# Two attention blocks on one core: another hand-written order for TensorE in the first block

## The chip, the cores and the metric

The kernel runs on one core of a Trainium2 chip. The metric is the device time of one execution in microseconds (us). Five engines work beside each other, each through its own queue in order: TensorE (PE) multiplies matrices into PSUM, VectorE (DVE), ScalarE (ACT) and GpSimd (POOL) work elementwise, and SyncE (SP) issues the DMA transfers. They wait for each other through semaphores.

## The reference

Two attention blocks, A and B, work on inputs of their own, and their outputs stand side by side:

```python
B, S, D = 1, 2048, 512            # both blocks
H = 32; Dh = D // H               # 32 heads of 16
qkv = (x @ wqkv).reshape(B, S, 3, H, Dh).transpose(2, 0, 3, 1, 4)
scores = einsum("bhqd,bhkd->bhqk", q, k) * Dh ** -0.5
# A alone: key j counts for query i only where 0 <= i - j < 256
p = softmax(scores)
o = einsum("bhqk,bhkd->bhqd", p, v)
out = o.transpose(0, 2, 1, 3).reshape(B, S, D) @ wo
# result: concatenate([A, B], axis=-1), float32
```

## The kernel before

All is computed to float32's precision: an operand of a projection is split into a rounded part and its rest, and three products stand for one. The heads are taken in groups of four (`g`, 8 groups), the queries in chunks of 512 (`c`, 4 chunks). A pair (g, c) is a unit. Block A has 32 units, block B 32.

The program has a first block, in which all of block A's attention runs together with the projections of A and of B, and a second block, which is B's attention with the output projections. The change touches the first alone. Its work for TensorE comes in kinds, each with a letter:

- `p`: one projection of 512 tokens or 128 value rows on the full array, 12 matmuls of 512 columns one after the other (line 309).
- `g`: a quarter of two projections side by side, one on each half of the array's rows: 12 matmuls as 6 simultaneous pairs (line 444). Four `g` make two projections. They need two PSUM banks until the last quarter.
- `m`: the scores of one query tile of 128 for two heads, from which the row maxima are taken (line 607): two simultaneous half-array matmuls of up to 384 columns into two banks. DVE then masks and reduces them (lines 616 and 617; line 612 for the first two tiles), which frees the banks. The last of these letters are the first maxima of block B (line 561).
- `e`: the same for block B's first unit, on operands loaded early.
- `t`: two transposes of a unit's negated maxima (line 681). ACT evicts them and two DMAs bring them as rows into the operand of the scores.
- `s`: scores of two heads for one step of a unit (line 717), half-array matmuls into two banks. ACT takes the exponential of each head out of PSUM (line 724), and POOL clears what the window masks (line 735).
- `w`: the probabilities of a step times the values (line 764), all 128 rows with 17 columns a head, four heads side by side in a bank of their own.

So `g`, `m`, `e` and `s` use two halves of the array's rows, `p`, `w` and `t` all 128. PSUM has eight banks: seven go round among `p`, `g`, `m`, `t` and `s`, and one is kept for `w`.

A unit is 8 `m`, a `t`, 6 `s` and 3 `w`. The order is written out by hand: `ORDER_A` (lines 75 to 83) is a string of 761 such letters, and `ORDER_P` (lines 60 to 65) names the 96 projections in the order in which `p` and `g` take them. `Bk21` is block B, keys, heads 16 to 23, tokens 512 to 1023; `v` names a row tile of the values instead. The loop at line 1122 takes the letters one by one and emits their instructions. The loads that SP issues are not in the strings: the kernel keeps a list of loads and reckons times for the emitted work (class `Model`), and a load is emitted when its operands and its buffer are ready by that reckoning. So another string also moves the DMAs.

A projection of queries or keys goes on from PSUM: ACT evicts it (line 392), POOL splits it in two instructions (lines 403 and 404) into one of two `st` tiles, SP stores that to DRAM (line 411), and later loads take it by heads into the operands `oq` and `opk` (lines 489 and 473) on which `m` and `s` work. A value projection is evicted by ACT into one of two `vst` tiles (line 508), stored (line 517) and loaded as `vt` (line 525), which `w` reads.

Of the kernel before, what the change touches and what calls it, by code (L numbers as in the profile page):

```python
# [57 lines left out]
FILL = 16  # L58
WARM = 22
ORDER_P = (  # L60
# [4 lines left out]
    "Bq20 Bq12 Bk30 Bk31 Bk10 Bq33 Bq30 Bq31 Bk32 Bq32 Bk33 Bk21 ").split()  # L65
WAKE = 200
GAP_V = 1500
PIECE = 4
# [4 lines left out]


ORDER_A = (
    "pppppppppppmmmmpmmgmgmptmgmgmmpmsgmsgmmpmsgmsgmwtsmgmsgmmpmsgsmgmtwwmmmpsmgmsgmswwmsgmsgmmpmssptwsmg"
    "msgmswsmgsmgmmwwmgmsgmstwmsgmsgmmwtsgmsgmswmsgmsgmswmmmpssmtwwmspmsmwssmgsmgmswtmsgsmgmwsmswssmwmmmp"
    "mtmswmsswmsmpsmmpsmwtmmmpsmswmmspmsmwsmsmwwtmsmsmsmpmsmtwsmsmwsmmswssmwmmspmmswsmwtsmgmsgmswsmgsmtgm"
    "mwsmwsmmswsmsmpsmmwmswtmsmwsmmmpmsssmmwsmsmwtmmmpsmswmsmsmwtsmsmwsmmpmmswsmtwmmmpmsgmsgmswtsmgmswpsm"
    "gsmwwmsgmmgmpmsgmsgsmwwtsmgmsgmswsmgsmgmmwtsgsmgsmwwmsgmsgmgsmgmswsmgmmgmwsmwtmsgmsgmswtmsgsmgmswwsm"  # L80
    "gmsgmswsmgsmgsmtwwmmmpmsmpmsmwsmmswtmsgmsgmswsmgsmgsmwmsmtwsmmswssmwmmmpmssmtwswmmmpmsgsmgsmwwmsgsmg"
    "etwmmmpmsgmsgmswsegsmgegesgmswsmgesgemtwmmpmsmwmswmsgsmgestwmsgesgmmpemmpmsmwwtemmpsmgmsgsmwmgegsewm"
    "mmpesstwmgmsgeswsmgsmgsmwesgsmgsmwmgsmgmswesmpsmmwtwmmmpmmmwp")
LAND = 400
LAND_V = 0
LGAP = 2500
# [1303 lines left out]
```

## Time and profile before

| what | value |
|---|---|
| median of 3 runs | 1776.09 us (1775.74 to 1776.34) |
| profiled execution: its own time, and its span | 1775.31 us, 1773.6 us |
| TensorE busy | 1756.7 us, 99% of the span |
| VectorE, ScalarE, GpSimd busy | 1527.2, 1402.7 and 650.5 us |
| first projection to the second block's first matmul | 6.60 to 514.88 us |
| granted TensorE clock | 1.00 throughout |

The lines of the profile group instructions by the line of the kernel, the engine and the tiles that they write and read. A row of the timeline is a start, a length, the engine, the line, the tiles, the shape and how many instructions were merged. A matmul's end is modelled and matmuls overlap, so TensorE looks busy nearly all the time, its short waits too. What it really takes is read from one start to the next.

### The profile page before, as it was taken

Reading aid. Unit: us, or ns where it says so; the run is one execution under the profiler, and the core shown is the slowest. Engines: PE = TensorE matmul, PEld = TensorE weight load, DVE = VectorE, ACT = ScalarE, POOL = GpSimd, SP = SyncE. Lnnn points to the kernel's source line nnn. Section 1 sums busy time; section 2 is a strip of 40 time slices with the busy share of each in tenths; the row PEclk is TensorE's granted clock in tenths of the full one; section 3 lists DMA queues with packets and bytes.
Section 4 is the critical chain, followed back from the end, with each engine's and each line's share of the span. In section 5 each row is a group of like instructions: output and inputs, shape, how many; then the busy total and the mean of one; then the engine's idle time right before and its main releaser. Section 6 shows DMA issues by size and latency. Waiting matters only on the chain.

```text
span 1773.6 us, 38893 instructions
## 1 busy us (share of the span) xinstructions
PE 1756.7 (99%) x14783; PEld 912.8 (51%) x14783; DVE 1527.2 (86%) x2386; ACT 1402.7 (79%) x2749; POOL 650.5 (37%) x1334
## 2 busy tenths in 40 slices
PE   8999999999999999999999999999999999999999
PEld 6776657767764444444444444444444344444446
DVE  4756786677789999999999999999999999999921
ACT  4366776665569888888889999999999999999894
POOL 0378888665755441222210123231102322121420
PEclk9999999999999999999999999999999999999999
DMA  8866767645663223111310311120031131010012
GB/s 261 203 204 202 213 206 224 176 147 170 196 182 107 67 85 89 41 41 41 83 37 17 77 29 30 49 60 17 17 78 35 30 65 38 17 39 25 20 44 102
DMA packets 129355, 166.78 MB, mean 94 GB/s; under 512 B 23205, under 2 KB 59045, under 8 KB 129157
## 3 DMA queue, kind: packets, MB, share of 16 engines
q1 hardware_dynamic: 129168, 164.31, 31.7%
q8 instruction: 116, 1.90, 0.5%
q14 instruction: 71, 0.57, 0.1%
HBM read 94.49 MB, written 68.19 MB: 92 GB/s over the span
## 4 chain that ended last, share of the span: by engine, by line
PE 92%; DVE 4%; ACT 1%; POOL 1%; DMA 1%; issue 1%; SPq 0%; POOLq 0%; ACTq 0%; DVEq 0%
PE ps_all L749 28%; PE ps_all L561 18%; PE ps_all L717 18%; PE ps_all L444 11%; PE ps_all L309 8%; PE ps_all L764 4%; PE ps_all L607 3%; DVE mt L564 3%; ACT p L724 1%; DMA in<-xT_A 1%; DVE nm L617 1%; PE ps_all L681 1%; DVE ps_all L616 0%; SPq L489 0%; DMA ld<-od 0%
## 5 line engine op out<-in xcount | busy, mean ns | idle before, releaser
L724 ACT ACTIVATE p<-ps_all 128x512 f32<-128x512 f32 x2432 | 1263.2, 597 | 202.7 <-PE ps_all L717 129.1
L564 DVE TENSOR_REDUCE mt<-ps_all 128x1 f32<-128x512 f32 (+1 forms) x1658 | 1212.7, 805 | 33.3 <-PE ps_all L561 28.5
L717 PE MATMUL ps_all<-oq,opk 51*128 51x512 f32 (+2 forms) x2752 | 757.3, 401 | 3.7 <-ACT p L724 2.0
L561 PE MATMUL ps_all<-opk,oq 48*128 48x512 f32 x2016 | 660.6, 435 | 0.0
L749 PE MATMUL ps_all<-p,vt 128*17 128x512 f32 (+1 forms) x5488 | 571.0, 490 | 0.0
L717 PEld LDWEIGHTS ps_all<-oq,opk 51*128 51x128 f32 x2752 | 386.0, 185 | 218.5 <-ACT p L724 142.9
L561 PEld LDWEIGHTS ps_all<-opk,oq 48*128 48x128 f32 x2016 | 304.1, 184 | 272.6 <-DVE mt L564 164.7
L735 POOL TENSOR_SCALAR_AFFINE_SELECT p<-p 128x256 f32<-128x256 f32 x480 | 179.9, 410 | 107.7 <-ACT p L724 104.3
L749 PEld LDWEIGHTS ps_all<-p,vt 128*17 128x17 f32 x5488 | 93.6, 95 | 214.1 <-issue 201.3
L616 DVE COPY_PREDICATED ps_all<-mone,ps_all 128x256 f32<-128x256 uint16 x224 | 95.3, 425 | 82.1 <-PE ps_all L607 75.4
L617 DVE TENSOR_REDUCE nm<-ps_all 128x2 f32<-128x512 f32 x224 | 155.2, 693 | 7.7
L633 POOL TENSOR_TENSOR mu<-mt 128x16 f32<-128x16 f32 x31 | 6.9, 223 | 411.4 <-DVE mt L564 411.4
L635 POOL TENSOR_TENSOR mu<-mt,mm 128x16 f32<-128x16 f32 x62 | 13.8, 222 | 388.1 <-DVE mt L564 388.1
L444 PE MATMUL ps_all<-x,w 64*128 64x512 f32 x720 | 119.0, 392 | 0.0
L444 PE MATMUL ps_all<-w_o,x_o 64*128 64x512 f32 x576 | 110.0, 394 | 0.0
L309 PE MATMUL ps_all<-x,w 128*128 128x512 f32 x408 | 102.6, 400 | 1.5 <-ACT x L257 0.8
L764 PE MATMUL ps_all<-p,vt 128*17 128x384 f32 (+2 forms) x1408 | 94.1, 387 | 0.1
L607 PE MATMUL ps_all<-opk,oq 48*128 48x384 f32 (+2 forms) x512 | 91.0, 361 | 1.2 <-DVE nm L617 0.3
L803 POOL TENSOR_TENSOR rd<-ld,minus 128x32 f32<-128x32 f32 x15 | 81.9, 5461 | 19.5 <-DMA ld<-od 19.5
L444 PEld LDWEIGHTS ps_all<-x,w 64*128 64x128 f32 x720 | 84.2, 185 | 8.6
L392 ACT ACTIVATE raw<-ps_all 128x512 f32<-128x512 f32 x56 | 32.3, 596 | 70.2 <-PE ps_all L309 55.3
L309 PEld LDWEIGHTS ps_all<-x,w 128*128 128x128 f32 x408 | 74.1, 188 | 23.8 <-ACT p L724 2.8
(81 smaller groups left out, 1046.6 us busy)
## 6 DMA issues: line engine op xcount, KB each, us to landing
parts<-st SPq DMA_DIRECT2D x64, 512.0 KB
oq<-parts SPq DMA_DIRECT2D x128, 128.0 KB
opk<-parts SPq DMA_DIRECT2D x128, 128.0 KB
od<-ou SPq DMA_DIRECT2D x64, 256.0 KB
vd<-vst SPq DMA_DIRECT2D x32, 272.0 KB
oq<-parts SPq DMA_DIRECT2D x128, 64.0 KB
opk<-parts SPq DMA_DIRECT2D x128, 64.0 KB
t<-od SPq DMA_DIRECT2D x32, 256.0 KB
```

The source lines that it names most:

```text
L309: nc.tensor.matmul(ps, l(u), r(v), start=start and k == 0, stop=stop and k == n - 1)
L444: op = nc.tensor.matmul(ps[a ^ turn], l(u)[rows], r(v)[rows], start=turn == q == 0, stop=turn == 1 and q == 11)
L561: nc.tensor.matmul(ps[:, a - lo], q[rows, 128 * qt:128 * qt + 128], k[rows, kc * QC:kc * QC + QC], start=True, stop=True)
L564: op = nc.vector.tensor_reduce(out=m[:, kc, lo:lo + len(sides), r, qt], in_=ps, axis=AX.X, op=ALU.max)
L607: nc.tensor.matmul(two[:, a, 0:w], opq[b, g, c][rows, r, 128 * qt:128 * qt + 128], opk2(g)[rows, r, t0:t1], start=True, stop=True)
L616: nc.vector.copy_predicated(two[:, :, 256:384], later, two[:, :, 0:128])
L617: op = nc.vector.tensor_reduce(out=m[:, :, r, qt, 0], in_=two[:, :, 128:384], axis=AX.X, op=ALU.max)
L717: nc.tensor.matmul(ps[x][:, col:col + n1], opk2(g)[rows, pr, 128 * k:128 * k + 128], opq[b, g, c][rows, pr, q0:q0 + n1], start=True, stop= ...
L724: op = nc.scalar.activation(p[:, a0 + x, :w], ps[x][:, :w], AF.Exp, scale=SCALE)
L735: nc.gpsimd.affine_select(out=v, in_=v, pattern=[[0, 2], [sign, 128]], compare_op=ALU.is_ge, fill=zero_fill, base=base, channel_multiplier ...
L749: nc.tensor.matmul(o[32 * j:32 * j + VW, q0:q1], vt[(g // 2) % 2][:, kt, vc:vc + VW], pts[1, g, c, kt, j // 2][:, j % 2, q0:q1], start=kt ...
L764: nc.tensor.matmul(o[32 * j:32 * j + VW, q0:q0 + w], vt[(g // 2) % 2][:, kt, vc:vc + VW], pts[b, g, c, m, j // 2][:, j % 2, col:col + w], ...
```

## The change

Both strings are new from a certain letter on. The first 31 letters of `ORDER_A` and the first 16 names of `ORDER_P` stay. Nothing else is changed: there are as many letters of each kind (280 `m`, 192 `s`, 96 `g`, 96 `w`, 48 `p`, 33 `t`, 16 `e`), each projection is named once, and the instructions that they emit are the same in number and size. Counting `w` and `t` as one kind, `p` as another and the half-array letters as a third, the string changes kind 259 times, where it was 242.

```diff
 ORDER_P = (
-    "Aq00 Ak00 Ak01 Av11 Av02 Av03 Aq01 Av01 Ak02 Av21 Av13 Aq02 Av12 Av00 Aq03 Ak03 Av20 Av10 Av33 Ak20 Av32 "
...
+    "Aq00 Ak00 Ak01 Av11 Av02 Av03 Aq01 Av01 Ak02 Av21 Av13 Aq02 Av12 Av00 Aq03 Ak03 Av33 Av32 Av23 Av10 Aq12 "
...
 ORDER_A = (
-    "pppppppppppmmmmpmmgmgmptmgmgmmpmsgmsgmmpmsgmsgmwtsmgmsgmmpmsgsmgmtwwmmmpsmgmsgmswwmsgmsgmmpmssptwsmg"
...
+    "pppppppppppmmmmpmmgmgmptmgmgmmpsmgmsgmmpmsgsmgmwmmtpmsgmsgmswwsmgsmgmtpsmgmsgmswsmgmsgmmwpmmtpsmwsmg"
...
```

Of what the two strings do to TensorE's queue, two places near 196 and 244 us of the execution before are shown. `opk` with `oq` in that order is an `m` (L607), the other way round an `s` (L717), `p_..` with `vt` a `w` (L764), `ident` with `nm` a `t` (L681), `x` with `w_` a projection.

The first place is in TensorE's queue after the values of unit (2, 0)'s second and third step. Before:

```order
L764 MATMUL ps_all<-p_2_0_2_1_2446,vt_78 17x256 x2
L681 LDWEIGHTS nm_74
L681 MATMUL ps_all<-ident,nm_74 32x128
L607 MATMUL ps_all<-opk_75,oq_2_3_2210 128x384 x2
L717 MATMUL ps_all<-oq_2_1_1854,opk_75 128x256 x4
L717 MATMUL ps_all<-oq_2_1_1854,opk_75 128x384 x2
L717 MATMUL ps_all<-oq_2_1_1854,opk_75 128x128 x2
L309 MATMUL ps_all<-x_2_0_239,w_3_0_1298 128x512 x3
```

After the change:

```order
L764 MATMUL ps_all<-p_2_0_1_1_2376,vt_78 17x384 x2
L717 MATMUL ps_all<-oq_2_1_1869,opk_75 128x256 x4
L607 MATMUL ps_all<-opk_75,oq_2_3_2211 128x384 x2
L764 MATMUL ps_all<-p_2_0_2_0_2441,vt_78 17x256 x2
L764 MATMUL ps_all<-p_2_0_2_1_2455,vt_78 17x256 x2
L717 MATMUL ps_all<-oq_2_1_1869,opk_75 128x384 x2
L717 MATMUL ps_all<-oq_2_1_1869,opk_75 128x128 x2
L309 MATMUL ps_all<-x_2_0_239,w_3_1_1238 128x512 x3
```

Rows that repeat are left out. Before, the letters there are `wwtmsmsmsmp`: both `w` together, and then four `m` and three `s` without another kind between them. After, they are `wsmwssmp`: the second `w` stands between an `m` and two `s`.

The second place is in TensorE's queue around the projection after unit (3, 1)'s first `w`. Before:

```order
L607 MATMUL ps_all<-opk_75,oq_4_0_3090 128x128 x2
L717 MATMUL ps_all<-oq_3_1_2604,opk_76 128x384 x2
L717 MATMUL ps_all<-oq_3_1_2604,opk_76 128x128 x2
L717 MATMUL ps_all<-oq_3_2_2732,opk_76 128x128 x2
L717 MATMUL ps_all<-oq_3_2_2732,opk_76 128x384 x2
L607 MATMUL ps_all<-opk_75,oq_4_0_3090 128x256 x2
L764 MATMUL ps_all<-p_3_1_1_0_3170,vt_78 17x256 x2
```

After the change:

```order
L607 MATMUL ps_all<-opk_75,oq_4_0_3084 128x128 x2
L309 MATMUL ps_all<-x_3_0_343,w_3_1_1238 128x512 x3
L717 MATMUL ps_all<-oq_3_1_2613,opk_76 128x384 x2
L717 MATMUL ps_all<-oq_3_2_2743,opk_76 128x128 x2
L717 MATMUL ps_all<-oq_3_2_2743,opk_76 128x384 x2
L607 MATMUL ps_all<-opk_75,oq_4_0_3084 128x256 x2
L764 MATMUL ps_all<-p_3_1_1_0_3166,vt_78 17x256 x2
```

Before, `msssmm` follows the projection up to the next `w`; after, one of the `m` has gone ahead of the projection, and `msssm` follows it.

In the second block TensorE's queue is the same, instruction for instruction.

More of the change, by code (lines that the diff above doesn't have):

```diff
@@ L60 @@
 ORDER_P = (
[4 rows of a table removed]
-    "Bq20 Bq12 Bk30 Bk31 Bk10 Bq33 Bq30 Bq31 Bk32 Bq32 Bk33 Bk21 ").split()
[4 rows of a table added]
+    "Bk13 Bk33 Bk31 Bk32 Bq31 Bq30 Bq11 Bq32 Bq33 Bk10 Bk30 Bq20").split()
 WAKE = 200
@@ L75 @@
 ORDER_A = (
-    "pppppppppppmmmmpmmgmgmptmgmgmmpmsgmsgmmpmsgmsgmwtsmgmsgmmpmsgsmgmtwwmmmpsmgmsgmswwmsgmsgmmpmssptwsmg"
[L77 to L83, printed above, removed]
+    "pppppppppppmmmmpmmgmgmptmgmgmmpsmgmsgmmpmsgsmgmwmmtpmsgmsgmswwsmgsmgmtpsmgmsgmswsmgmsgmmwpmmtpsmwsmg"
+    "msgmswsmgsmgmmtwmgmgmswsmgmsgmswmmswssmgmmgstwmsgsmgmwmmtpsmswwsmmpsmswmsgmsgmswgtmsgmwssmwmsswmsmpm"
+    "mswmsswtmmspmmmpsmswtmmmpsmswmmmpmsmswmsmsmtwsmwssmpmtmswsmsmwsmmswmsmswmmmpsmwtmswssmgsmgmswsmgmsgm"
+    "twssmwmmswsmsmpsmmwstmwmsmwmsmmmpmsssmwmsmtwsmmmpsmstwmsmsmwsmmswsmmpmsmtwmswmmmpsmgsmgmswmsgsmwtpms"
+    "gmswsmgmsgmmwpmsgsmgmwwtmsgmsgmswsmgsmgmswmsgmsgmmwtwsgmsgmgsmgmswsmgmmgmtwmswmsgmsgmswtmsgmsgsmwwms"
+    "gmsgmswsmgsmgmmpmsmwsmtwmsmpmmswsmtwmsgsmgsmwmsgmsgmswmmswtssmswmmmpssmwmsmwsmtwmmmpmsgsmgsmwwmsgsmg"
+    "mtwemmpmsgsmgeswsmgsmgegsmgeswsmgesgmmtwmmpmsmtwsmwsmgmmgswsmgmsgempesswtemmpmswemmpsmgmsgswemgmgmtw"
+    "emmpseswesgmsgsewmgmsgmswmsgesgmswsegmgmswmmspmmswtwmmmpmmmwp")
 LAND = 400
```

6 rows, old and new, of the table ORDER_P are left out of this document.

## The prediction

> **What bounds the kernel now.** I read the page first (engines with busy time, share and instructions), then the chain of work that ended last in two stretches of the first block, then TensorE's timeline there.
>
> ```profile
> span 1773.6 us, 38893 instructions
> ...
> PE 1756.7 (99%) x14783; PEld 912.8 (51%) x14783; DVE 1527.2 (86%) x2386; ACT 1402.7 (79%) x2749; POOL 650.5 (37%) x1334
> ...
> PEclk9999999999999999999999999999999999999999
> ...
> 6.60 0.50 PE L309 MATMUL ps_all<-x,w 128*128 128x512 f32 x1 [0.78 <-ACT x L257]
> ...
> 514.88 0.50 PE L717 MATMUL ps_all<-oq,opk 51*128 51x512 f32 x2
> ```
>
> TensorE bounds it, at full clock. The change can move only what lies between the first projection (6.60 us) and the second block's first scores (514.88): 508.3 us. TensorE's queue in the 1258.7 us behind that is untouched. The matmuls are the same ones, so there are two terms: turns, the time lost where the array passes between whole and halves, and waits, in which the next letter's banks or operands are not ready.
>
> Chain, 190 to 270 us, then 270 to 515.4 us:
>
> ```profile
> by line: PE ps_all L309 20.0%; ACT p L724 14.8%; PE ps_all L717 14.0%; PE ps_all L764 12.4%; PE ps_all L607 9.5%; DVE nm L617 7.9%; PE ps_all L444 5.5%; issue 5.0%; DVE ps_all L616 4.9%; DVE nm L668 1.5%; ACT x L257 1.3%; DVE junk L612 0.9%
> ...
> by line: PE ps_all L444 34.1%; PE ps_all L309 19.3%; PE ps_all L764 18.3%; PE ps_all L717 11.2%; PE ps_all L607 10.4%; PE ps_all L561 4.8%; PE ps_all L681 0.7%; DVE nm L617 0.6%; DVE ps_all L616 0.3%; ACT raw L392 0.2%; issue 0.1%; PE ps_al
> ```
>
> In the earlier stretch the exponentials (L724) and the maxima (L616, L617) hold a good quarter of the chain; later almost nothing. Waits sit where projections are `p`, in lumps of 3 us, and few `g` part the `m` from the `s`.
>
> **Turns.** From start to start on TensorE's timeline:
>
> ```profile
> 163.52 1.06 PE L764 MATMUL ps_all<-p,vt 128*17 128x256 f32 x16
> 164.51 1.04 PE L607 MATMUL ps_all<-opk,oq 48*128 48x384 f32 x6
> ...
> 180.93 1.06 PE L764 MATMUL ps_all<-p,vt 128*17 128x256 f32 x16
> 181.81 0.23 PE L681 MATMUL ps_all<-ident,nm 128*32 128x128 bf16 x2
> 181.97 0.79 PE L607 MATMUL ps_all<-opk,oq 48*128 48x384 f32 x6
> 182.68 3.01 PE L309 MATMUL ps_all<-x,w 128*128 128x512 f32 x12
> 185.62 0.44 PE L717 MATMUL ps_all<-oq,opk 51*128 51x384 f32 x2
> 185.91 0.34 PE L607 MATMUL ps_all<-opk,oq 48*128 48x384 f32 x2
> 186.09 0.34 PE L717 MATMUL ps_all<-oq,opk 51*128 51x384 f32 x2
> 186.35 0.84 PE L764 MATMUL ps_all<-p,vt 128*17 128x384 f32 x8
> ...
> 393.11 0.23 PE L681 MATMUL ps_all<-ident,nm 128*32 128x128 bf16 x2
> 393.13 0.86 PE L764 MATMUL ps_all<-p,vt 128*17 128x384 f32 x8
> ...
> 9.49 17.75 PE ps_all L309 x77
> ```
>
> A 384-column half-array pair takes 0.18 (185.91 to 186.09) among its own kind, 0.29 as the first after a projection (185.62 to 185.91: +0.11) and 0.26 as the last before a `w` (186.09 to 186.35: +0.08). A `w` of four 256-column passes takes 0.88 before a `t` and 0.99 before an `m` (+0.11). A `t` takes 0.16 before an `m`, 0.02 before a `w` (+0.14). A `p` between half-array letters takes 2.94; 77 of its matmuls one after the other (the last row, of the chain) run at 0.23, twelve at 2.77, so its two ends cost some 0.2.
>
> Counting the neighbours in both strings, before to after:
>
> - into halves: from `w` 65 to 78, at 0.22; from `t` 19 to 11, at 0.25; from `p` 35 to 36, at 0.21;
> - out of halves: to `w` 70 to 74 and to `t` 14 to 22, at 0.08; to `p` 35 to 29, at 0.18;
> - among whole-array letters: `t` or `w` to `p` 2 to 8, estimated at 0.22 from the ends of the two (`t` to `p` occurs nowhere before); `p` to `t` 2 to 1, at 0.1; `w` with `t` nothing.
>
> 13 x 0.22 - 8 x 0.25 + 0.21 + 12 x 0.08 - 6 x 0.18 + 6 x 0.22 - 0.1 = +2.2 us. Priced letter by letter to the nanosecond, the turns go from 42.4 to 44.8 us: I take **+2.4**. Where a turn falls ahead of a letter that must wait anyway it costs nothing; the bound below is that half do: +1.2.
>
> [...]
>
> **Waits.** Start to start less the price, over all letters, the waits before come to 31.6 us (434.3 of matmuls, 42.4 of turns and 31.6 make the 508.3): 7.3 in the first 42 letters, which hardly change, 3.8 up to 186 us, 12.8 from there to 279 us, 7.7 behind. What one looks like, inside `smsmsm`:
>
> ```profile
> 195.68 0.44 PE L607 MATMUL ps_all<-opk,oq 48*128 48x384 f32 x2
> 195.96 0.41 PE L717 MATMUL ps_all<-oq,opk 51*128 51x256 f32 x4
> 196.20 0.34 PE L607 MATMUL ps_all<-opk,oq 48*128 48x384 f32 x2
> 196.57 0.38 PE L717 MATMUL ps_all<-oq,opk 51*128 51x256 f32 x1
> 197.19 0.38 PE L717 MATMUL ps_all<-oq,opk 51*128 51x256 f32 x2 [0.23 <-ACT p L724]
> 197.41 0.43 PE L607 MATMUL ps_all<-opk,oq 48*128 48x384 f32 x1
> ...
> L724 ACT ACTIVATE p<-ps_all 128x512 f32<-128x512 f32 x320 | 172.4, 600 | 54.9 <-PE ps_all L717 44.3 <-PE ps_all L607 5.4 <-POOL p L735 2.5
> L616 DVE COPY_PREDICATED ps_all<-mone,ps_all 128x256 f32<-128x256 uint16 x224 | 95.3, 425 | 82.1 <-PE ps_all L607 75.4 <-ACT ou L775 4.0 <-PE ps_all L717 1.5
> L617 DVE TENSOR_REDUCE nm<-ps_all 128x2 f32<-128x512 f32 x224 | 155.2, 693 | 7.7
> ```
>
> An `s` took 0.24 (195.96 to 196.20), the next one 0.84 (196.57 to 197.41): its second bank came free with an exponential. An `m` needs DVE for 1.1 us (425 + 693 ns), an `s` ACT for two exponentials of 600, each for two of seven banks, while TensorE takes 0.2 to 0.3 for either. So what counts is how many follow without a `p`, `g` or `w`. I cut the string at those and sorted the runs by (maxima, score pairs), behind the 42nd letter; the waits of the runs are 22.2 us:
>
> - (2,2): 10 runs, 6.6 us in all (0.39 to 0.81); 6 after.
> - (3,3) and (4,3): one each, 1.5 and 1.7; none after.
> - (3,2): one, 1.0; two after. (3,1): one, 0.8; one after.
> - (1,2): 11, 1.8; 15 after. (2,1): 20, 2.2; 20 after.
> - (1,1): 115, 5.1; 111 after. (3,0): 15, 0.9; 13 after. Smaller: 29, 0.5; 38 after.
> - Only after, one each: (1,3), between (1,2) at 0.16 and (3,3) at 1.5, taken near the first, 0.4; (2,3), between 0.66 and 1.5, 1.0; (4,1), between 0.8 and 1.7, 1.0.
>
> The (4,3) run is the first place shown of the change, the (3,3) run the second. At the means: 4.0 + 2.0 + 0.8 + 2.4 + 2.2 + 5.0 + 0.8 + 0.6 + 2.4 = 20.1, or -2.1. If each run of the change takes instead the wait of the run before with the same letters behind the same kind, where there is one, the waits fall by 3.5. I take **-2.8**. Bounds: every (2,2) and new run at its lowest, 17.7 (-4.5); at its highest, 23.5 (+1.3).
>
> **Sum:** +2.4 - 2.8 = -0.4 us. On the profiled execution's 1775.31 us (span 1773.6, 1.7 around it) that is 1774.9; its time lies 0.8 below the median of the runs, so against that **1775.7 us**. Its own range is -4.5 + 1.2 to +1.3 + 2.4: 1772.8 to 1779.8.
>
> **Rivals.** One, *slower, by an operand that comes late*. `Aq10`, the queries of unit (2, 0), now ends 24.2 us of priced TensorE work ahead of the first `m` that reads it, where it was 35.5; `Aq11` 26.3 where it was 36.2. The way to `oq`, in the longest legs that the trace shows:
>
> ```profile
> 185.73 0.60 ACT L392 ACTIVATE raw<-ps_all 128x512 f32<-128x512 f32 x1 [2.43 <-PE ps_all L309]
> 196.99 0.38 SPq L411 DMA_DIRECT2D parts<-st  x1
> ...
> 58.32 0.36 SPq L411 DMA_DIRECT2D parts<-st  x1
> 64.22 2.72 SPq L489 DMA_DIRECT2D oq<-parts  x4
> ...
> 382.48 1.82 SPq L489 DMA_DIRECT2D oq<-parts  x4
> 387.91 0.85 PE L607 MATMUL ps_all<-opk,oq 48*128 48x384 f32 x6
> ...
> 196.53 0.61 POOL L403 CAST st<-raw 128x512 fp32r<-128x512 f32 x1 [2.98 <-DMA parts<-st]
> ```
>
> Eviction to store 11.3 (POOL stood waiting for an `st` tile, 2.98 of it, and SP's queue after that), store to loads 5.9, four loads 2.7, landed at most 3.6 behind the last issue (384.30 to 387.91): 23.5, and some 24 from the projection's end. So at the worst it just arrives. It decides if POOL's queue, or SP's, is a few us longer there. Then all of that is TensorE's wait, because `m` comes in order and the `s` behind it stand too: 5 us gives 1780.7. Against it: these legs fell on different tiles, and the planner emits each load when its operand is due. Chance 0.17.
>
> Two, *faster, because waits hang together*: three of the (2,2) runs and the (4,3) run follow each other between 193 and 208 us, each inheriting a queue on ACT and DVE. Broken up, the 12.8 us of 186 to 279 us would fall by some 6, not 2.8: -6 + 1.8 of turns gives 1771.9. Against it: ACT and DVE have the same work in that stretch, and runs like `smsm`, `smms` and `msmsm` stay. Chance 0.26.
>
> That the strings don't do what they say is excluded by the built queues.
>
> **How the numbers follow.** Forecast 0.57, faster rival 0.26, slower rival 0.17. About 0.2% (3.6 us) is what counts as different from no change: the forecast lies within, both rivals outside. The range reaches to both rivals: 1771.0 to 1780.0, which leaves out the slower half of the one and the far end of the other.
>
> **What would show it.** Right: the second block's first scores near 514.5 us and 1258.7 us behind it; half-array letters after `w` still 0.22 dearer; in 190 to 270 us L724 and L617 with a smaller share of the chain, and no more than 10 us of waits there. Wrong: a wait on `oq` (from a DMA, over 1 us) near 150 us; `w` waiting for L735; a second block that is longer by more than 0.5 us, as its operands are loaded in the first.

## The result and the profile after

The changed kernel takes 1786.41 us, the median of six executions (1782.47 to 1787.66), against 1776.09 us (1775.07 to 1776.38) before: a ratio of 1.0053, with a 95% interval of 1.0042 to 1.0064. The forecast was 1775.7 us and no difference; the change makes the kernel slower by 0.5% (10.3 us between the medians), and the time lies outside the range.

The head of the page, and TensorE's timeline at the end of the first block, of the changed kernel:

```profile
span 1783.7 us, 38903 instructions
...
PE 1766.4 (99%) x14783; PEld 915.5 (51%) x14783; DVE 1527.3 (86%) x2386; ACT 1402.2 (79%) x2749; POOL 650.4 (36%) x1334
...
PEclk9999899999999999999999999999999999999999
...
524.89 0.50 PE L717 MATMUL ps_all<-oq,opk 51*128 51x512 f32 x2
```

The second block's first scores start at 524.89 us instead of 514.88, and 1258.8 us lie behind them, where it was 1258.7. So all that is lost is lost in the first block, as the prediction's frame had it. What is new is one digit of the row of the clock: an 8 in the fifth slice, at 178 to 223 us. TensorE's timeline there, after the change:

```profile
200.57 3.04 PE L309 MATMUL ps_all<-x,w 128*128 128x512 f32 x12
204.81 0.29 PE L607 MATMUL ps_all<-opk,oq 48*128 48x128 f32 x1 [1.21 <-DMA oq<-parts]
205.64 0.30 PE L607 MATMUL ps_all<-opk,oq 48*128 48x128 f32 x1 [0.53 <-DMA oq<-parts]
...
209.74 1.91 PE L764 MATMUL ps_all<-p,vt 128*17 128x256 f32 x16
211.57 0.80 PE L717 MATMUL ps_all<-oq,opk 51*128 51x256 f32 x4
```

The `m` at 204.81 (letter 252; letters are counted from 0) is the first of unit (3, 0). Its two halves wait for their queries, one after the other; by the starts and the prices of the letters they cost 2.1 us. The kernel before has no wait on a transfer there; its letter 252 starts right behind the projection and takes both halves at once:

```profile
201.97 0.33 PE L607 MATMUL ps_all<-opk,oq 48*128 48x128 f32 x2
```

And in the changed kernel, 5 us later, a `w` of four passes needs 1.83 us from start to start (209.74 to 211.57) instead of 0.88 to 0.99. The windows of time, which give TensorE's busy time second and the granted clock third from the end, say why:

```profile
204.09:207.50 3.41, 2.16 (x26) 1.22 (x26) 1.46 (x9) 1.20 (x4) 2.35 (x3) 1.00 0.69 225
207.50:210.91 3.41, 3.41 (x28) 2.23 (x28) 1.73 (x8) 2.65 (x6) 2.31 (x7) 0.50 0.62 192
...
217.74:221.16 3.42, 3.42 (x26) 1.70 (x26) 1.75 (x6) 1.93 (x4) 2.54 (x7) 0.50 0.40 116
221.16:224.57 3.41, 3.41 (x20) 2.44 (x18) 2.97 (x6) 0.15 (x1) 0.97 (x1) 1.00 0.06 23
```

From 207.50 to 221.16 us, 13.65 us, TensorE is granted half its clock. Before, it had the whole clock from end to end (mean 1.000).

Why the queries are late stands in SP's queue, first before, then after the change:

```profile
189.52 0.38 SPq L782 DMA_DIRECT2D od<-ou  x1
189.94 0.42 SPq L525 DMA_DIRECT2D vt<-vd  x1
...
191.07 1.32 SPq L525 DMA_DIRECT2D vt<-vd  x2
...
194.41 2.38 SPq L489 DMA_DIRECT2D oq<-parts  x4
```

```profile
191.97 0.41 SPq L782 DMA_DIRECT2D od<-ou  x1
...
193.26 2.11 SPq L525 DMA_DIRECT2D vt<-vd  x3
...
196.50 1.24 SPq L525 DMA_DIRECT2D vt<-vd  x1
197.80 0.67 SPq L796 DMA_DIRECT2D ld<-od  x1
198.56 2.38 SPq L489 DMA_DIRECT2D oq<-parts  x4
```

Two loads are let go by letters. The four loads of values for group pair 2 (L525) wait for unit (1, 3)'s last `w`, whose store (L782) is issued at 191.97 instead of 189.52. The loads of unit (3, 0)'s queries (L489) wait for a free `oq` buffer, so for unit (2, 0)'s last `s`, which is letter 236 instead of 234. Before, the queries were issued at 194.41, ahead of the fourth load of values; after, behind all four, at 198.56, while the `m` that reads them could have started only 1.5 us later than before: at 203.5, when its projection was done, instead of 201.97. The chain of waits over 192 to 207 us shows the same; its rows are a start, a length and what ran:

```profile
by line: DMA vt<-vd 37.5%; DMA oq<-parts 32.9%; SPq L525 10.2%; DVE nm L617 4.7%; PE ps_all L764 4.3%; PE ps_all L607 3.7%; issue 2.4%; DVE ps_all L616 2.3%; PE ps_all L717 1.9%; DVE nm L668 1.4%; PE ps_all L681 1.1%; SPq L810 0.4%
...
194.92 5.62 DMA vt<-vd
...
200.56 4.94 DMA oq<-parts
```

By the prediction's own measure (starts less the price of each letter) the 10.0 us at the end of the first block divide so: start-up, up to letter 28, which the strings share, -1.7; turns +2.4; late queries +2.1; halved clock about +4.2; other waits, which are what is left, +3.0. The size of the halved clock is from the letters 260 to 290, which took 23.3 us here, and 19.1 in the second run below at whole clock. The executions of the changed kernel agree in kind: one took 1782.47 us at a mean clock of 0.999, three took 1787.34 to 1787.66 at 0.995.

### The profile page after: what moved, and what is told of

The parts are those of the page before. It is cut to its first block, busy times and chain, and to the rows that moved or that the text cites. A ratio compares the mean times of both kernels' runs of the same rounds, so it can differ in the third digit from the quotient of the medians.

```text
span 1783.7 us, 38903 instructions
## 1 busy us (share of the span) xinstructions
PE 1766.4 (99%) x14783; PEld 915.5 (51%) x14783; DVE 1527.3 (86%) x2386; ACT 1402.2 (79%) x2749; POOL 650.4 (36%) x1334
## 4 chain that ended last, share of the span: by engine, by line
PE 89%; DVE 4%; DMA 2%; POOL 1%; ACT 1%; issue 1%; SPq 1%; POOLq 0%; ACTq 0%; DVEq 0%
PE ps_all L749 28%; PE ps_all L717 18%; PE ps_all L561 18%; PE ps_all L444 11%; PE ps_all L309 7%; PE ps_all L764 4%; DVE mt L564 3%; PE ps_all L607 3%; DMA in<-xT_A 1%; ACT p L724 1%; PE ps_all L681 1%; DMA vd<-vst 1%; DMA vt<-vd 0%; DVE nm L617 0%; DMA parts<-st 0%
## 5 line engine op out<-in xcount | busy, mean ns | idle before, releaser
L724 ACT ACTIVATE p<-ps_all 128x512 f32<-128x512 f32 x2432 | 1262.8, 597 | 208.7 <-PE ps_all L717 138.7
L717 PE MATMUL ps_all<-oq,opk 51*128 51x512 f32 (+2 forms) x2752 | 758.2, 402 | 2.0 <-ACT p L724 1.6
L717 PEld LDWEIGHTS ps_all<-oq,opk 51*128 51x128 f32 x2752 | 387.4, 186 | 217.5 <-ACT p L724 141.5
L735 POOL TENSOR_SCALAR_AFFINE_SELECT p<-p 128x256 f32<-128x256 f32 x480 | 179.9, 409 | 119.9 <-ACT p L724 119.7
L617 DVE TENSOR_REDUCE nm<-ps_all 128x2 f32<-128x512 f32 x224 | 155.2, 693 | 7.7
L444 PE MATMUL ps_all<-x,w 64*128 64x512 f32 x744 | 131.4, 392 | 0.4 <-ACT p L724 0.4
L764 PE MATMUL ps_all<-p,vt 128*17 128x384 f32 (+2 forms) x1408 | 98.5, 395 | 0.6 <-POOL p L735 0.5
L607 PE MATMUL ps_all<-opk,oq 48*128 48x384 f32 (+2 forms) x512 | 94.0, 369 | 4.4 <-DMA oq<-parts 1.7
L444 PEld LDWEIGHTS ps_all<-x,w 64*128 64x128 f32 x744 | 92.6, 185 | 10.6 <-ACT p L724 1.4
L444 PE MATMUL ps_all<-w_v,x 64*128 64x512 f32 x408 | 87.3, 391 | 0.0
```

What stands on the lines that cost most here:

```text
L444: op = nc.tensor.matmul(ps[a ^ turn], l(u)[rows], r(v)[rows], start=turn == q == 0, stop=turn == 1 and q == 11)
L607: nc.tensor.matmul(two[:, a, 0:w], opq[b, g, c][rows, r, 128 * qt:128 * qt + 128], opk2(g)[rows, r, t0:t1], start=True, stop=True)
L617: op = nc.vector.tensor_reduce(out=m[:, :, r, qt, 0], in_=two[:, :, 128:384], axis=AX.X, op=ALU.max)
L717: nc.tensor.matmul(ps[x][:, col:col + n1], opk2(g)[rows, pr, 128 * k:128 * k + 128], opq[b, g, c][rows, pr, q0:q0 + n1], start=True, stop= ...
L724: op = nc.scalar.activation(p[:, a0 + x, :w], ps[x][:, :w], AF.Exp, scale=SCALE)
L735: nc.gpsimd.affine_select(out=v, in_=v, pattern=[[0, 2], [sign, 128]], compare_op=ALU.is_ge, fill=zero_fill, base=base, channel_multiplier ...
```

## The experiments

Each run stands against executions of the kernel before on its own chip.

| run | median us | before | ratio (95%) |
|---|---|---|---|
| changed kernel | 1786.41 | 1776.09 | 1.0053 (1.0042 to 1.0064) |
| queries first | 1785.92 | 1776.88 | 1.0048 (1.0033 to 1.0063) |
| wait filled | 1784.37 | 1776.88 | 1.0036 (1.0023 to 1.0049) |
| before, queries late | 1780.22 | 1776.88 | 1.0017 (1.0006 to 1.0029) |
| new ends, old middle | 1777.48 | 1776.88 | 1.0003 (0.9993 to 1.0012) |
| new middle | 1782.69 | 1777.13 | 1.0037 (1.0023 to 1.0051) |
| queries first, values later | 1778.70 | 1777.13 | 1.0014 (1.0005 to 1.0023) |
| new letters, old projections | 1789.88 | 1777.13 | 1.0071 (1.0059 to 1.0083) |
| old letters, new projections | 1783.22 | 1777.13 | 1.0030 (1.0020 to 1.0040) |
| 17 more changes to halves | 1783.74 | 1776.44 | 1.0044 (1.0032 to 1.0057) |
| two pieces of the change | 1777.80 | 1776.44 | 1.0012 (1.0002 to 1.0023) |
| two pieces, values later | 1781.77 | 1776.44 | 1.0038 (1.0025 to 1.0051) |
| lump broken up | 1777.66 | 1776.44 | 1.0008 (0.9999 to 1.0017) |

The theory after the traces: late queries make TensorE wait, the idle time halves its clock, and this is most of the loss. The rivals: the order itself costs it (its bank waits, or the fall of the clock with them), or the turns cost more than they were priced at.

### Queries ahead of the values

```diff
 list_("v", lambda u=u: done["w"] >= u - 2 * NQC and (u < NA or ne == len(early))
+      and (u != 16 or ("qd", 0, 3, 0) in ready),
```

> The changed kernel, with the load of the queries of unit (3, 0) put ahead of the four loads of values for group pair 2 on SP's queue. Theory (the late queries make TensorE wait some 2 us at letter 252, and its clock is then halved for some windows): no wait on these queries over 0.3 us, granted clock 1.000, and the 7.4 us that the changed kernel loses between letters 231 and 273 are gone: 1776.1 + 10.0 - 7.4 = 1778.7, between 1777.5 and 1780.0. Rival (the order itself, its bank waits and turns between whole and half array, costs the 10 us, and the clock falls because of that order): the time stays at 1784 or more and the clock below 1. Second rival (the turns were priced at a quarter of their cost): 1784 or more with the clock at 1.000.

The time did not fall: 1785.92 us. One wait went and another came, in the waits of TensorE up to 525 us and in the windows:

```profile
PE ps_all L717 <- DMA oq<-ntr: 2.5, 1, 2.5
...
205.56:208.97 3.41, 1.26 (x19) 0.41 (x17) 0.72 (x6) 1.60 (x3) 3.33 (x5) 1.00 1.06 366
208.97:226.04 17.07, 16.34 (x97) 9.71 (x98) 9.79 (x25) 7.88 (x15) 9.29 (x21) 0.50 0.44 144
```

`oq<-ntr` is the row of maxima that unit (2, 2)'s `s` needs (line 688). It came 2.5 us late, with a DMA share of 1.06 over 205.56 to 208.97 us, when the loads of values stood right behind the queries, and the clock was halved for 17.07 us. As it stood, the expectation failed. The run told neither theory from rival, as it had moved the crowd, not removed it.

### The wait filled with matmuls

```diff
+            for k in range((16, 5)[a] if (g, c, qt, j) == (3, 0, 0, 0) else 0):
+                y = 1 if a else k % 2
+                z = slice(ROW[y], ROW[y] + KS)
+                nc.tensor.matmul(two[:, y, 0:384], opq[0, 2, 1][z, 0, 0:128], opk2(2)[z, 0, 0:384], start=True, stop=True)
             nc.tensor.matmul(two[:, a, 0:w], opq[b, g, c][rows, r, 128 * qt:128 * qt + 128], ...
```

The added matmuls' results are overwritten by the maxima's own scores.

> The changed kernel, with 21 matmuls of no use on old operands, some 2.2 us of half-array work, put ahead of the first maxima of unit (3, 0), into the banks that these write afterwards. The queries are as late as before. Theory (idle time is what halves the clock): the wait is filled with work, the clock stays at 1.000, and the time is that of the kernel with early queries plus the 2 to 2.5 us of the wait: 1780.5 to 1782. Rival (the wait and the order cost it, the clock is not a matter of this gap): 1785 to 1788 with a clock near 0.995.

In this kernel L610 is the filling and L611 the `m`. Timeline and windows:

```profile
201.64 2.47 PE L309 MATMUL ps_all<-x,w 128*128 128x512 f32 x10
204.03 1.68 PE L610 MATMUL ps_all<-opk,oq 48*128 48x384 f32 x16
205.55 0.22 PE L611 MATMUL ps_all<-opk,oq 48*128 48x128 f32 x1
205.56 1.04 PE L610 MATMUL ps_all<-opk,oq 48*128 48x384 f32 x5
...
202.70:206.10 3.40, 3.40 (x28) 2.87 (x27) 0.54 (x3) 1.09 (x2) 3.26 (x6) 1.00 0.99 276
206.10:223.20 17.10, 15.93 (x168) 9.53 (x170) 12.96 (x38) 11.95 (x24) 12.66 (x26) 1.00 0.51 153
```

The queries are as late as before, TensorE does useless work instead of nothing, and its clock stays whole (1.00 from 206.10 to 223.20 us) through the stretch in which it was halved (0.50 from 207.50 to 221.16 us in the changed kernel). So idle time, not the order, brought the clock down there. The letters 260 to 290 take 19.1 us instead of 23.3. The time, 1784.37, lies 2.4 us above the expected range: in the profiled execution another wait, 1.4 us ahead of a `g` at 298 us, was followed by one window at half clock (299.81 to 303.22 us), which this run had not aimed at. That is not all of it: four executions at a mean clock of 1.000 took 1782.18 to 1785.09 us.

### Queries late in the kernel before

```diff
-list_("q", lambda u=u: done["s"] >= u - 3, stored(b, g // 2, 0, (c,)), load_q_at, b, g, c)
+list_("q", lambda u=u: done["s"] >= u - 3 and (u != 12 or len(todo_a) <= 761 - 240), stored(...
```

> The kernel before, with nothing changed but the place of the load of the queries of unit (3, 0), which now stands behind the fourth load of values and one load of x on SP's queue, some 4.5 us later. Theory: TensorE waits 2 to 3 us for these queries at letter 252 near 202 us, and its clock is halved for one to four windows of 3.4 us: 1776.1 + 2.5 + 1.3 to 6.7 = 1780 to 1785, clock 0.995 to 0.999. Rival (the clock fell because of the new order): only the wait is added, 1778 to 1779, clock 1.000.

Of the 2 to 3 us of wait that were meant, 0.8 came about (the `m` at 201.31 us waited 0.84 us for `oq<-parts`), and the clock of the profiled execution is 1.000. The median is 3.3 us above before, with executions from 1777.6 us at clock 1.000 to 1785.5 at 0.996. The wait stayed below what was meant; this run decides nothing on the clock.

### New ends and an old middle; the new middle alone

```diff
-ORDER_A = changed string
+ORDER_A = changed[:163] + before[163:345] + changed[345:]   (projections likewise; the second kernel is the mirror)
```

> The changed strings in letters 1 to 163 and from 346 on, the strings before in the 182 letters between (both strings hold the same letters and the same projections up to each of these cuts). Theory: the middle holds the late queries and so most of the loss. By the two traces the outer parts lose 1.4 us up to letter 164 (the start-up, which the strings share, left out) and 1.7 us behind letter 346, 1.75 us of it turns: 1776.1 + 3.1 = 1779.2, between 1777.5 and 1780.5, clock 1.000. Rival (the turns cost what is lost): 1.75 of the 2.4 us of priced turns lie in the outer parts, so 1776.1 + 0.73 x 10 = 1783.4.

> The strings before, with letters 164 to 345 and their projections from the changed strings; the mirror of the kernel with new ends and an old middle. Theory: the late queries of unit (3, 0) and the halved clock behind them lie in this stretch and come with it: 1776.1 + 10.0 - 1.4 = 1784.7, between 1782 and 1787, clock 0.995 to 0.999. Rival (the loss needs the outer parts, which make the stretch begin 1 to 2 us later against the transfers): 1777 to 1779 and clock 1.000.

The new ends cost 0.6 us (1777.48), less than the 3.1 expected, and the interval holds no difference too; the new middle alone costs 5.6 (1782.69), at the low end of what was expected. Its trace repeats the one of the changed kernel, with a longer wait and five windows at half clock. This profiled execution is one of the slower ones (1787.95 us, mean clock 0.995); the one at a mean clock of 1.000 took 1781.14, still 4.0 us above the kernel before.

```profile
205.63 0.29 PE L607 MATMUL ps_all<-opk,oq 48*128 48x128 f32 x1 [2.16 <-DMA oq<-parts]
...
202.71:206.12 3.41, 1.08 (x6) 0.54 (x4) 0.16 (x1) 0.71 (x2) 3.33 (x6) 1.00 0.92 272
206.12:223.19 17.07, 16.67 (x115) 8.95 (x115) 8.25 (x29) 9.80 (x19) 10.47 (x23) 0.50 0.45 144
```

So the larger part of the loss lies in letters 164 to 345, though only 0.6 of the 2.4 us of turns lie there. The rival that blamed the turns would have put 7 us into the ends.

### Queries first, and the values well behind

```diff
 list_("v", lambda u=u: done["w"] >= u - 2 * NQC and (u < NA or ne == len(early))
+      and (u != 16 or ("qd", 0, 3, 1) in ready),
```

> The changed kernel, with the four loads of values for group pair 2 put behind the loads of the queries of unit (3, 1), so that neither the queries of unit (3, 0) nor the maxima rows of units (2, 2) and (2, 3) queue behind them. In the kernel with only the queries put first the wait on these went, but the maxima rows of unit (2, 2) came 2.5 us late at 207 us and the clock fell for 17.1 us. Theory (a stretch of idle TensorE halves the clock, wherever it comes from): no wait on a transfer over 0.5 us between 190 and 230 us, clock 0.999 or 1.000, and 2.4 us of turns and some 2 us of small waits stay: 1779 to 1781.5. Rival (the new order itself lets the clock fall): 1784 or more, clock 0.998 or below.

1778.70 us, 1.6 us above the kernel before on the same chip, where the changed kernel stood 10.3 above: one condition on four loads takes 8.7 us away, and not a letter is changed. The timeline and the windows:

```profile
201.20 3.03 PE L309 MATMUL ps_all<-x,w 128*128 128x512 f32 x12
204.16 0.33 PE L607 MATMUL ps_all<-opk,oq 48*128 48x128 f32 x2
...
202.70:206.10 3.40, 3.40 (x33) 2.15 (x31) 1.85 (x12) 2.61 (x7) 3.40 (x8) 1.00 0.89 247
206.10:223.20 17.10, 15.44 (x164) 9.18 (x160) 12.44 (x32) 12.39 (x25) 13.71 (x28) 1.00 0.62 187
```

The `m` follows its projection at once, and the clock is whole (1.00). This settles what costs most of it: the late transfers, with the waits and the halved clock behind them. That the condition is a gain by itself is unlikely: the kernel with the lump broken up has it too and took 1777.66 us, and the one with the two pieces took 1781.77 with it and 1777.80 without. It was not run on the kernel before alone. In the traces, from letter 28 to the end of the block, 4.4 us stay against the kernel before: 2.4 of turns and 2.0 of small waits (27.7 us instead of 25.7). The spans of the two profiled executions differ by 2.7 us and the medians by 1.6; the start-up, 1.2 us longer in the trace of before, is part of that.

### One of the strings alone

The changed `ORDER_A` with the `ORDER_P` of before, and the reverse.

> The changed string of letters with the projections in the order before. Theory: the turns and the late queries come from the letters (unit (2, 0)'s scores and unit (1, 3)'s weighted sums end later against the loads), so the time stays near that of the changed kernel: 1782 to 1788, clock 0.995 to 0.999. Rival (the order of the projections, through ScalarE's and GpSimd's work and the stores on SP's queue, makes the queries late): 1777 to 1780, clock 1.000.

> The string of letters before, with the projections in the changed order. Theory: no turn is added and no query is late: 1775.5 to 1778, as before. Rival (the order of the projections makes the loss): 1782 or more with a wait on queries or keys.

The letters alone lose 12.8 us, more than the theory had, and not in its place: in this trace, of the slowest of its executions, the same `m` waits 1.6 us, at 215 us, without a fall of the clock, but the first 28 letters end 5.5 to 6.1 us later than in the changed kernel and its variants (at 60.4 us instead of 54.3 to 54.9), and single windows at half clock stand at 10, 41 and 99 us. The projections alone lose 6.1 us, where at most 2 were expected: queries are late by 1.31 us at 406 us and a row of maxima by 0.71 right behind, and two windows are at half clock:

```profile
196.29:199.70 3.41, 2.38 (x24) 1.47 (x19) 2.97 (x7) 2.77 (x6) 3.41 (x9) 1.00 0.84 229
199.70:203.11 3.41, 3.41 (x13) 2.50 (x12) 2.53 (x7) 1.76 (x4) 2.99 (x8) 0.50 0.84 282
...
404.50:407.91 3.41, 1.38 (x14) 1.09 (x12) 1.23 (x7) 1.12 (x3) 1.53 (x4) 1.00 0.43 142
407.91:411.33 3.42, 3.42 (x28) 2.79 (x28) 0.60 (x4) 1.09 (x2) 0.00 (x0) 0.50 0.40 125
```

Neither half of the change is harmless, and the two losses do not add up: together the halves lose 10.3 us, not 18.9.

### The price of the turns

```diff
-"...smwtsmsmwsmm... wtsmgmswp... wwmsg..."
+"...smwstmsmwsmm... wstmgmswp... wmwsg..."   (17 such places)
```

> The kernel before, with 17 swaps of two neighbouring letters between 358 and 707: where two of w and t stand together, a maxima or score pair is put between them (once ahead of them). That makes 17 more changes from whole or quarter array to halves and 16 back, and moves nothing else. By the prices of the prediction the letters grow from 471.1 to 476.1 us. Theory (the turns were priced right, and in this stretch TensorE waits little): 1776.1 + 5.1 = 1781.2, between 1780 and 1782.5. Rival (turns fall into waits that are there anyway, as the lower bound of the prediction had it): 2.5 us, 1778.6. Second rival (turns cost about three times as much, which would explain the loss of the changed kernel without any late load): 1790.

1783.74 us: 7.3 more instead of 5.1. A new half-array letter between two `w`, in the timeline:

```profile
293.34 0.84 PE L764 MATMUL ps_all<-p,vt 128*17 128x384 f32 x8
294.11 0.44 PE L607 MATMUL ps_all<-opk,oq 48*128 48x384 f32 x2
294.48 0.63 PE L764 MATMUL ps_all<-p,vt 128*17 128x256 f32 x8
```

It takes 0.37 us (294.11 to 294.48), where a letter among its own takes 0.18: 0.19 for its two ends, as priced. Over the five letters around each swap, 14 of the 17 places take 0.0 to 0.5 us longer than before, 0.3 in the middle, which is the price; three take 1.0 to 1.2, because a letter there waited. From letter 346 on the trace takes 8.9 us more than before: 5.1 of turns, and 3.8 of waits. The price per turn holds. What the expectation left out is that a moved letter also moves waits.

### Pieces of the change

The first two kernels have the letters of before but for 333 to 345 and 525 to 579, the third but for 231 to 272; the second and third also have the condition on the values shown above.

> The strings before, with only two pieces of the changed letters, 333 to 345 and 525 to 579, in which the changed kernel's trace gains 0.8 and 1.3 us on that before; in the second lies the run of three maxima and three score pairs that the change breaks up. Projections as before. Theory (what a piece gains, it gains alone): 1776.1 - 2.1 = 1774.0. Rival (the gains were start-up and transfer luck of the trace): 1775.5 to 1776.7.

> The kernel with the two pieces, and the four loads of values for group pair 2 behind the loads of the queries of unit (3, 1), as in the changed kernel where this took the waits away. Theory (the kernel before has no wait on a transfer in 190 to 230 us to lose): no gain over the kernel with the two pieces alone, 1773 to 1775. Rival (the space on SP's queue takes away the weak stretches in which the clock of the kernel before falls in some executions): 0.5 to 1.5 us less.

> The strings before, with only the changed letters 231 to 272, which break up the run of four maxima and three score pairs near 196 us, and with the four loads of values later, so that no query is late there. The table of the prediction gives these 42 letters 3.9 us of waits instead of 4.1, the prediction took some 0.7 us less for the broken run alone, and the turns cost 0.6 more: 1776.1 + 0.6 - 0.2 to -0.7 = 1776.0 to 1776.5. Rival (the waits follow VectorE's and ScalarE's load and not the runs; in the changed kernel without late queries the same letters waited 0.6 us more): 1777.3. Rival, the one of the prediction (waits hang together): 1773 or less.

The two pieces do not gain on before but lose 1.4 us (1777.80), and with the values later 5.3 (1781.77), where a faster kernel was expected. In both profiled executions the first 28 letters, which no edit touches, ended 1.8 us later than in the one of before. The run of three maxima and three score pairs stands in the first piece, not in the second as the expectation says. By starts and prices that piece waited 1.9 us instead of 2.2, and the 24 letters behind it, which were not changed, 3.2 instead of 1.9. In the changed kernel it had been the same, 1.3 and then 3.1. It looks as if the wait moved on, but that is not shown: in the run of the kernel before with late queries, whose letters are all those of before, the same 24 letters take 16.7 us from start to start instead of 15.3, as much longer as in the run of the two pieces (16.6).

The broken lump, letters 231 to 272, waited 5.1 us instead of 4.8, and its kernel took 1777.66, close to the 1777.3 of the rival that puts the waits down to VectorE's and ScalarE's load; its interval holds no difference too. The gain of the prediction's rival is excluded.

No version beat the kernel before.

## Why the prediction was wrong, by its own steps

- **The frame held.** TensorE bounds the kernel, and the loss is in the first block alone. The second block kept its length to 0.1 us.
- **Turns, +2.4: held.** The letters' prices in the changed kernel's trace add up to that, and the 17 swaps confirmed the price of one turn. That they fall into waits anyway (the lower bound) was not seen.
- **Waits, -2.8: failed.** This is the term of the sum that was wrong. With the late transfer taken away the waits behind letter 28 rose by 2.0 us, and with it by 9.3. The step that failed inside it is the table of runs: it took a lump's wait to belong to its letters. The lump at 196 us, broken up alone, kept its wait (5.1 us in its 42 letters instead of 4.8); breaking up the run of three and three near 250 us took 0.3 us off that piece, and the unchanged letters behind waited 1.3 longer, as they did in a run with the old letters. And the letters 403 to 524, the same in both, waited 1.8 us in the kernel before and 3.4 in the one with the broken lump, 79 us and more behind the edit of the letters: a bound of -4.5 to +1.3, made of one trace's runs, did not hold what such a shift does.
- **The slower rival: right in kind, wrong in place.** It said that an operand would come late, priced the delay one for one, and looked at how early `Aq10` and `Aq11` end. Those were in time: there is no wait on `oq` near 150 us. The queries that came late, of unit (3, 0), are the other heads of `Aq10` and had been projected long before; what delayed them was the buffer that they load into, and the four loads ahead of them on SP's queue. The prediction's measure, from projection to use, cannot see that. The right one starts at the last `s` of the unit four back.
- **The clock was missing.** The prediction noted "at full clock" and kept it for the changed kernel, so a fall of the clock is no term of its sum. Behind the late queries the clock was 0.50 for 13.65 us, and a wait of 2.1 us cost about 6.3; with the wait filled the clock there stayed at 1.00.
- **The faster rival fell.** Waits do not hang together in the way it assumed: the broken lump gained nothing.
- **What would show it.** The condition "a wait on `oq` from a DMA, over 1 us" came true, 55 us later than named. So did, once and for 0.5 us, a `w` that waits for L735. A sign of being right came true too, and did not mean a gain: in the run with the values later, over 190 to 274 us, L724 holds 10.7% of the chain instead of 14.8, and L617 5.0 instead of 7.9, while the waits rose.

## What to carry to other kernels

When the order of work is changed, check for every load the event that lets it go (a buffer that comes free) and what is queued ahead of it, not only when its data are ready. A queue that had slack before may have none after a shift of 2 us (here the store of unit (1, 3) went out 2.5 us later, and the loads of the queries 4.2). A wait of TensorE can cost more than its length (here 2.1 us cost about 6.3, though waits of 0.8 and 1.6 us in other runs cost no clock), and before blaming a new order, take away the late transfers: here that gave back 8.7 of 10.3 us.

## What the runs showed of the hardware

The clock fell by stretches of one length or a multiple of it, and not by idle time alone. The stretches at half clock in these traces (the end of each program left out) are 3.41, 13.65 or 17.07 us long, one, four or five times 3.41, and the granted clock in them is 0.50. With the old letters and new projections two of them begin at 199.70 and 407.91 us, 208.21 us apart, which is 61 times 3.413. In the 3.41 us ahead of the falls shown here TensorE was not idle throughout: it was busy for 1.08 us (the new middle) to 2.16 us (the changed kernel, both above), or even for 2.67 to 2.70. The next rows are of the kernel before and of that with 17 more changes, whose queue is the same up to there. Both windows hold the same wait (0.7 us of L717 for L724) and the same busy time (2.67 us); the second began at another point of the work, and held 31 matmuls, all of half-array or narrow letters, instead of 18, projections among them:

```profile
196.53:199.94 3.41, 2.67 (x18) 1.88 (x17) 3.27 (x8) 3.17 (x7) 3.33 (x7) 1.00 1.00 298
199.94:203.35 3.41, 3.38 (x36) 2.43 (x34) 2.17 (x10) 1.88 (x5) 3.41 (x10) 1.00 0.95 326
```

```profile
194.94:198.35 3.41, 2.67 (x31) 1.64 (x22) 3.00 (x6) 2.98 (x7) 2.83 (x5) 1.00 1.00 266
198.35:201.76 3.41, 3.41 (x13) 2.50 (x10) 2.62 (x8) 1.70 (x4) 3.41 (x11) 0.50 0.96 313
```

Two windows of projections alone held more idle time, 1.71 and 1.75 us. The one with 1.70 us of work kept the clock (the kernel before, first row); the one with 1.67 lost it (the two pieces, second fence):

```profile
36.10:39.51 3.41, 1.70 (x8) 1.06 (x7) 2.08 (x4) 1.87 (x4) 0.00 (x0) 1.00 0.77 269
39.51:42.92 3.41, 3.15 (x17) 2.10 (x15) 0.75 (x5) 0.60 (x1) 0.00 (x0) 1.00 0.95 278
```

```profile
8.33:11.75 3.42, 1.67 (x6) 1.18 (x7) 1.90 (x3) 2.32 (x5) 0.00 (x0) 1.00 1.03 384
11.75:15.16 3.41, 3.41 (x10) 2.64 (x9) 3.10 (x5) 2.04 (x4) 0.00 (x0) 0.50 1.04 405
```

What parts the windows of a pair is not shown: no run varied one thing alone. Two windows of the two pieces with values later fit neither the busy time nor the kind of the matmuls: the first, with three matmuls of projections in it and 2.70 us of work, lost the clock (second row), and the other, with none and 2.64 us (third row), kept it.

```profile
198.92:202.34 3.42, 2.70 (x15) 1.65 (x16) 3.32 (x7) 3.41 (x7) 3.42 (x9) 1.00 0.87 264
202.34:205.75 3.41, 3.41 (x10) 2.67 (x9) 1.27 (x4) 0.63 (x1) 3.39 (x7) 0.50 0.87 277
...
209.16:212.57 3.41, 2.64 (x28) 1.38 (x30) 1.96 (x10) 2.94 (x7) 3.32 (x7) 1.00 0.55 147
```

One kernel's executions differ in their clock, too: the kernel before ran in 1774.2 to 1774.9 us at a mean of 1.000 and in 1780.5 at 0.997, beside each other. Why is not shown. Open is also why half clock lasted four or five windows ahead of 221 to 226 us and one elsewhere. Where it lasted longer, scores and weighted sums filled it, but for the last window with the queries first, which held a projection; where it lasted one, projections (`p` or `g`) ran in it, but in one case (256.95 to 260.36 us, the two pieces with values later) it was scores and weighted sums, too.

The start-up differs by several us between programs that begin with the same letters and projections: letter 28 started between 54.3 and 60.4 us. That is more than the forecast's whole effect.
